# One-bank PSUM tiles in the block products of a mixture-of-experts kernel, with the row staging in two parts

## The chip, the cores and the metric

One core of one Trainium2 chip runs the whole program. The metric is device time in microseconds (us), from the program's start to its end on that core, as the median of several executions. The kernel before has a median of 686.16 us. The rows below come from one execution under the hardware profiler, whose own time was 684.45 us.

## What is computed

Linear attention without a softmax for 8 batches and 8 heads (576 rows of 64 columns), an RMS normalization of every head's row, and a mixture of experts in which each of the 4608 resulting rows of 512 columns goes to the best one of 8 experts:

```python
kv = np.einsum('bhsd,bhde->bhse', q, np.einsum('bhsd,bhse->bhde', k, v))   # then RMS norm, g_norm
x = attn_out.transpose(0, 2, 1, 3).reshape(B * S, H * D)                   # 4608 x 512
e_idx = np.argmax(x @ w_gate, axis=1)
for e in range(E):
    mask = e_idx == e
    h = np.maximum(x[mask] @ w1[e], 0.0)                                   # 512 -> 1024
    ye = h @ w2[e]                                                         # 1024 -> 512
    out[mask] = gate_w[mask, None] * eom[mask, e, None] * ye
```

All inputs and outputs are fp32, and the matrix products of the experts keep nearly that precision: an operand is split into a high and a low part (`hi`, `lo`), and a product is three matmuls (high by high, high by low, low by high).

## The kernel before

The first 110 us or so do the attention and the routing; rows are written to a buffer `xs` in DRAM, and lists of indices (`gidx`, `oidx`) say which rows an expert takes. The experts follow, ordered by their number of rows, in nine runs (`RUNS`): the first expert has two runs (256 and 436 rows), the others one each, of 672, 632, 608, 592, 576, 576 and 544 rows. A run gathers its rows, computes h (1024 x rows) and from it y, which a DMA writes to the rows of the output.

From the third run on, x @ w1 is made with Winograd's form of the 2 x 2 block product, `seven(i)`. For each of four chains c (256 of the 1024 columns of h) it issues seven products of six matmuls each (`product`, L458; two contraction blocks by three pairs of high and low parts), each n = rows / 2 columns wide. Their names are those of the operand blocks: 11, S3, 12, S2, S1 of chain c, and in between S4 and 22 of the chain before (`late3`, `late4`). Two accumulators hold a chain: `a` takes 11, S2, S1 and, while the next chain runs, S4, one on top of another; ScalarE copies its state to `sn` after the first three (L511, L521, L529). `d` takes S3 and later 22; VectorE reads it after each (L530, L496). VectorE's L518 adds the product 12 to the first of these copies. `split_h` writes a part of h: a relu on ScalarE (L482) gives the high part, VectorE (L485) the low one. The product 12 goes to one of two other banks (`y0`, `y1`), which the results of mm2 use too. `a` and `d` are the two banks of one PSUM tile:

```python
            ad = ps_b.tile([P, 2, 512], F32, name="hps", tag="big")
            a, d = ad[:, 0, 0:n], ad[:, 1, 0:n]
```

The pool `ps_b` has three such two-bank buffers; the staging of rows takes its tile `tps` from the same pool. Two banks are left for `ps_y`. The framework orders the accesses to a tile and inserts every semaphore wait; within the runs each of TensorE, ScalarE, VectorE and GpSimd executes its instructions in the order in which the program issues them.

`mm2(i, k, events)` makes y for one tile k of 128 rows: eight steps f of three matmuls of 512 columns (0.23 us each at full clock), then the evacuation by ScalarE (L588) and the indirect DMA from GpSimd (L589). The dictionary `events` hangs other work behind a step f of a tile, with `put(tile, step, function, ...)`. So while a run's mm2 is on TensorE, the next run is prepared: `sums_of` (sums of weight blocks, on GpSimd), `w_split` (high and low parts of those weights, ScalarE and VectorE), `x_stage(i + 1, k)` for k = 0, 1, 2 (two row tiles each: eight transposes on TensorE into `tps`, then copies, sums of blocks and their low parts on ScalarE and VectorE, in turns), the loads of weights (`wload`, SP's queue), and, in the last tile, the first chain of the next run. The gather of the next run's rows and `scale_rows` (GpSimd) are issued between the chains of the run before. `listing` is a list of small VectorE operations on rows that fit no expert's place; two of its pieces are issued per chain in the third and fourth run.

SBUF tiles for weights, rows and block sums come from one ring of 29 slots (`take` and `give`): whoever takes a slot waits for the last user of it.

Of the kernel before, what the change touches and what calls it, by code (L numbers as in the profile page):

```python
# [21 lines left out]
P = 128  # L22
# [113 lines left out]
def body(ctx: ExitStack, tc: tile.TileContext, kvm, rem, qT, wg, gn, w1, w2, kc, xs, tab, out):  # L136
# [24 lines left out]
    main = ctx.enter_context(ExitStack())  # L161
    mem = main.enter_context(tc.tile_pool(name="mem", bufs=1))
    psum = bass.MemoryType.PSUM
    ps_b = main.enter_context(tc.tile_pool(name="ps_b", bufs=3, space=psum))
    ps_y = main.enter_context(tc.tile_pool(name="ps_y", bufs=1, space=psum))
    loads = []
    kvp, mrp = (ps_y.tile([P, 512], F32, name=n, tag=t) for n, t in (("kvp", "y0"), ("mrp", "y1")))
    free = list(range(SLOTS - ROWS))
# [187 lines left out]

    wsum, wop, xop = {}, {}, {}

    def rest(i):

# [46 lines left out]
    def x_stage(i, k):  # L409

        p, _, C = RUNS[i]
        n, r = C // 2, rest(i)
        if k == 0:
            xop[i] = [hp.tile([P, 6, n], F32R, name=f"xb{j}") for j in range(2)]
            xop[i] += [mem.tile([P, 8, n], F32R, name="xT", tag=f"xT{j}") for j in range(2)]
        bh, bl, th, tl_ = xop[i]
        ps = ps_b.tile([P, 2, 512], F32, name="tps", tag="big")
        ts_ = tiles_of(i)
        for j, (t, c0, M) in enumerate(ts_[2 * k:2 * k + 2]):
            x = xg.pop((p, t))  # L420
            tl = cst.tile([P, 1], F32, name="tl", bufs=14)
            nc.vector.tensor_copy(tl[:M], x[:M, C_SCALE:C_SCALE + 1])
            tails[(p, t)] = tl
            for c in range(4):
                if k < 2:
                    o = ps[:, j, c * P:(c + 1) * P]
                else:
                    o = ps[:, c // 2, c % 2 * 256 + j * P:][:, 0:M]
                nc.tensor.transpose(o, x[:M, c * P:(c + 1) * P], ident[:M, :M])
            give(x)  # L430
        m, c0 = (P, k * P) if k < 2 else (r // 2, 2 * P)
        if k < 2:
            v = ps.rearrange("q b (c m a) -> q a c b m", c=4, a=2)
            part = lambda t, d: t[:, d, c0:c0 + m].rearrange("q d (b m) -> q d b m", b=2)
        else:
            v = ps.rearrange("q b (c m a) -> q a (b c) m", c=2, a=2)[:, :, :, 0:m]
            part = lambda t, d: t[:, d, c0:c0 + m]
        a, b = v[:, 0], v[:, 1]
        xt_ = take([P, 8, P], F32, "xt")
        xt = xt_[:, :, 0:m]  # L440
        if k < 2:
            xt = xt.rearrange("q d (b m) -> q d b m", b=2)
        V = nc.vector
        d1, d2 = slice(0, 2), slice(2, 4)
        nc.scalar.copy(xt[:, 6:8], b[:, d1])
        V.tensor_tensor(out=xt[:, 0:2], in0=xt[:, 6:8], in1=a[:, d1], op=ALU.subtract)
        V.tensor_tensor(out=xt[:, 4:6], in0=b[:, d2], in1=xt[:, 6:8], op=ALU.subtract)
        V.tensor_tensor(out=xt[:, 2:4], in0=b[:, d2], in1=xt[:, 0:2], op=ALU.subtract)
        V.tensor_tensor(out=xt[:, 6:8], in0=a[:, d2], in1=xt[:, 2:4], op=ALU.subtract)  # L449
        cs = slice(c0, c0 + m)  # L450
        for hi, lo, x in ((part(bh, slice(0, 4)), part(bl, slice(0, 4)), a),
                          (part(bh, slice(4, 6)), part(bl, slice(4, 6)), b[:, d2]),
                          (th[:, :, cs], tl_[:, :, cs], xt_[:, :, 0:m])):
            nc.scalar.copy(hi, x)  # L454
            V.tensor_tensor(out=lo, in0=x, in1=hi.bitcast(F32), op=ALU.subtract)  # L455
        give(xt_)

    def product(ps, W, X, start):  # L458
# [7 lines left out]
    def seven(i):  # L466

        nonlocal ny
        p, _, C = RUNS[i]
        n = C // 2  # L470
        st = {}
        S, V = nc.scalar, nc.vector

        T = half(i)
        C0 = C - T

        def split_h(c, f, a, x):

            h = hT[i][:, 2 * c + f]
            v = lambda o, k: h[:, o:o + 2 * k].rearrange("q (k a) -> q a k", a=2)[:, a]  # L480
            hh = v(0, n)
            S.activation(hh, x, AF.Relu)  # L482
            cut = C0 // 2
            for o, j0, j1 in ((C + T, 0, cut), (C, cut, n)) if T else ((C, 0, n),):
                V.scalar_tensor_tensor(out=v(o, j1 - j0), in0=x[..., j0:j1], scalar=0.0,  # L485
                                       in1=hh[..., j0:j1].bitcast(F32), op0=ALU.max, op1=ALU.subtract)

        def late3(c):
            a, d, sn, ct = st[c]
            product(a, w_of(c, "S4"), x_of(i, "22"), False)  # L490
            split_h(c, 0, 1, a)

        def late4(c):
            a, d, sn, ct = st.pop(c)
            product(d, w_of(c, "22"), x_of(i, "T4"), False)
            V.tensor_tensor(out=ct[:, 0:n], in0=d, in1=sn[:, 1], op=ALU.add)  # L496
            split_h(c, 1, slice(0, 2), ct[:, 0:2 * n].rearrange("q (a k) -> q a k", a=2))
            give(st.pop(("sn", c)))
            give(st.pop(("ct", c)))
            w_drop(c)  # L500

        for c in range(4):
            ad = ps_b.tile([P, 2, 512], F32, name="hps", tag="big")
            a, d = ad[:, 0, 0:n], ad[:, 1, 0:n]
            st["sn", c] = take([P, 1024], F32, "sn")
            st["ct", c] = take([P, 1024], F32, "ct")
            sn = st["sn", c][:, 0:3 * n].rearrange("q (s n) -> q s n", s=3)
            ct = st["ct", c][:, 0:3 * n]
            st[c] = (a, d, sn, ct)
            product(a, w_of(c, "11"), x_of(i, "11"), True)  # L510
            S.copy(sn[:, 0], a)  # L511
            yield
            product(d, w_of(c, "S3"), x_of(i, "T3"), True)
            yield
            b = ps_y.tile([P, DM], F32, name="hps2", tag=f"y{ny % 2}")[:, 0:n]
            ny += 1
            product(b, w_of(c, "12"), x_of(i, "21"), True)
            V.tensor_tensor(out=ct[:, 2 * n:3 * n], in0=b, in1=sn[:, 0], op=ALU.add)  # L518
            yield
            product(a, w_of(c, "S2"), x_of(i, "T2"), False)  # L520
            S.copy(sn[:, 1], a)  # L521
            yield
            if c:
                late3(c - 1)
                yield
                late4(c - 1)
                yield
            product(a, w_of(c, "S1"), x_of(i, "T1"), False)
            S.copy(sn[:, 2], a)  # L529
            V.tensor_tensor(out=ct[:, n:2 * n], in0=d, in1=sn[:, 2], op=ALU.add)  # L530
            if c == 0:
                hT[i] = hp.tile([P, 8, 2 * C], F32R, name="hT")
            split_h(c, 0, 0, ct[:, 2 * n:3 * n])
            yield
        late3(3)
        yield
        late4(3)
        xop.pop(i)
        yield
# [651 lines left out]
    with tc.manual_schedule(engines=MAN):  # L1191
# [12 lines left out]
        for i in range(len(RUNS)):  # L1204
# [7 lines left out]
            elif i == 1:  # L1212
                for f in range(8):
                    mm1(i, f)
                    if f % 2:
                        split(p, 2, f // 2)
                        drop(1, f // 2)
                        wload(p + 1, 1, f // 2)
                    if f == 2:
                        gather(i + 1)  # L1220
                    if f == 3:
                        scale_rows(i + 1)
                    if f == 6:
                        sums_of(p + 1, 0)
            else:

                for c in range(4):
                    if c:
                        begin(i, 6)
                        if change:  # L1230
                            wload(p + 1, 1, c - 1)
                        begin(i, 1)
                    split(p, 2, c)
                    if c == 1 and not last_run:
                        g_ = gather(i + 1)
                        if i + 2 == len(RUNS):
                            settle(g_)
                    if c == 2 and not last_run:
                        scale_rows(i + 1)
                    if c == 3 and change:  # L1240
                        sums_of(p + 1, 0)
                    next(listing, None)
                    next(listing, None)

# [11 lines left out]
                if change:  # L1256
                    put(order[0], 3, wload, p + 1, 1, 3)
            if change:
                for c in range(1, 4):
                    put(order[c - 1], 4, sums_of, p + 1, c)  # L1260
                for c in range(4):
                    put(order[min(c, T - 2)], 5 if c < T - 1 else 6, w_split, p + 1, c)
                for k in range(3):
                    put(order[k], 6, x_stage, i + 1, k)
                put(order[T - 1], 0, wload, p + 1, 2, 0)
                for f, n in ((1, 1), (3, 2), (5, 1), (7, 1)):
                    put(order[T - 1], f, begin, i + 1, n)
# [120 lines left out]
```

## Time and profile before

| | |
|---|---|
| median of the runs shown | 686.16 us |
| profiled execution, its own time | 684.45 us |
| its span, first to last instruction | 682.6 us |
| mean granted TensorE clock | 0.95 of 2.4 GHz |
| TensorE (PE) busy | 568.8 us, 83% |
| VectorE (DVE) busy | 395.1 us, 58% |
| ScalarE (ACT) busy | 293.9 us, 43% |
| GpSimd (POOL) busy | 261.8 us, 38% |

A busy share is an average over the attention, the chains and mm2, which have different limits; matmuls are pipelined, so that a busy TensorE need not be at its peak. What a change to the chains can be worth is read from the waits inside them.

### The profile page before, as it was taken

How to read it: one execution, taken by the hardware profiler on the slowest of the kernel's cores; microseconds unless marked ns; L12 is line 12 of the kernel's file. 1: busy time of each engine (PE TensorE's matmuls, PEld its weight loads, DVE VectorE, ACT ScalarE, POOL GpSimd, SP SyncE). 2: the span in 40 equal slices, each digit the busy share in tenths (PEclk: the TensorE clock that was granted, in tenths of full speed). 3: DMA queues.
4: the chain of work that ended last, by engine and by line, in shares of the span. 5: the costliest groups of instructions: out<-in, count | busy, mean ns of one | idle time of the engine just before them, and what ended most of it. 6: DMA issues, size and time to landing. Idle time of an engine off the chain costs nothing.

```text
span 682.6 us, 10867 instructions
## 1 busy us (share of the span) xinstructions
PE 568.8 (83%) x4052; PEld 476.2 (70%) x4052; DVE 395.1 (58%) x806; ACT 293.9 (43%) x583; POOL 261.8 (38%) x280
## 2 busy tenths in 40 slices
PE   8999999999487699779886978698868886888696
PEld 6888887588276577677676857676667676767674
DVE  1238988468736674547725683578256844784430
ACT  1577644235523354335524553455234533453321
POOL 2001431892425434165515461546154623662011
PEclk9899969999789999899889999997999899989999
DMA  8999988520144002341243015301530153013000
GB/s 283 385 417 415 400 335 329 179 83 16 47 146 135 32 15 94 125 138 42 72 163 119 32 62 182 118 31 62 179 119 32 57 170 122 32 52 135 1 17 39
DMA packets 28743, 92.34 MB, mean 135 GB/s; under 512 B 4082, under 2 KB 4210, under 8 KB 28688
## 3 DMA queue, kind: packets, MB, share of 16 engines
q1 hardware_dynamic: 21952, 71.63, 28.9%
q0 software_dynamic: 6304, 19.78, 8.7%
q8 instruction: 33, 0.54, 0.3%
q10 hardware_dynamic: 432, 0.21, 0.1%
q14 instruction: 22, 0.18, 0.1%
HBM read 72.41 MB, written 19.78 MB: 135 GB/s over the span
## 4 chain that ended last, share of the span: by engine, by line
PE 40%; DVE 21%; ACT 16%; issue 6%; POOL 1%; DMA 0%; POOLq 0%; ACTq 0%; DVEq 0%
PE hps L462 21%; PE yps L575 11%; DVE wl L387 6%; ACT hT L482 5%; DVE hT L485 4%; ACT whi L225 3%; PE yps L569 3%; DVE wlo L228 3%; PE hps L308 2%; PE yps L553 2%; DVE ct L496 2%; ACT y L588 2%; DVE xb L455 1%; ACT wh L386 1%; ACT xb L454 1%
## 5 line engine op out<-in xcount | busy, mean ns | idle before, releaser
L575 PE MATMUL yps<-whi,hT 128*128 128x512 f32 (+3 forms) x560 | 193.8, 410 | 18.9 <-ACT y L588 18.9
L462 PE MATMUL hps<-xT,wh 128*128 128x288 f32 (+5 forms) x448 | 101.2, 315 | 64.9 <-ACT sn L511 35.7
L575 PEld LDWEIGHTS yps<-whi,hT 128*128 128x128 f32 (+3 forms) x560 | 108.2, 193 | 47.2 <-ACT y L588 23.0
L589 POOL DMA_INDIRECT out<-y,oidx x42 | 50.7, 1207 | 226.3 <-ACT y L588 183.9
L462 PEld LDWEIGHTS hps<-xT,wh 128*128 128x128 f32 x448 | 74.2, 192 | 79.8 <-ACT sn L511 40.9
L575 PE MATMUL yps<-wlo,hT 128*128 128x512 f32 (+3 forms) x280 | 113.5, 405 | 0.1
L462 PE MATMUL hps<-xb,wh 128*128 128x288 f32 (+5 forms) x336 | 74.8, 311 | 14.0 <-ACT xb L454 8.9
L462 PEld LDWEIGHTS hps<-xb,wh 128*128 128x128 f32 x336 | 56.9, 195 | 18.4 <-ACT xb L454 9.3
L243 POOL DMA_INDIRECT xg<-xs,gidx x42 | 42.3, 1008 | 69.6 <-DVE ct L496 28.6
L462 PE MATMUL hps<-xT,wl 128*128 128x288 f32 (+5 forms) x224 | 68.4, 305 | 0.0
L482 ACT ACTIVATE hT<-ct 128x288 fp32r<-128x288 f32 (+11 forms) x56 | 34.5, 617 | 70.8 <-DVE ct L496 70.8
L485 DVE SCALAR_TENSOR_TENSOR hT<-ct,hT 128x256 fp32r<-128x256 f32 (+6 forms) x88 | 48.7, 583 | 22.9 <-ACT hT L482 22.9
L575 PEld LDWEIGHTS yps<-wlo,hT 128*128 128x128 f32 (+3 forms) x280 | 54.4, 194 | 10.7 <-DVE wlo L228 0.5
L521 ACT COPY sn<-hps 128x288 f32<-128x288 f32 (+5 forms) x28 | 11.5, 410 | 94.1 <-PE hps L462 94.1
L462 PE MATMUL hps<-xb,wl 128*128 128x288 f32 (+5 forms) x168 | 51.3, 306 | 0.0
L454 ACT CAST xb<-tps 128x512 fp32r<-128x512 f32 (+11 forms) x42 | 17.2, 409 | 77.1 <-DVE xt L449 63.6
L228 DVE TENSOR_TENSOR wlo<-wraw,whi 128x1024 fp32r<-128x1024 f32 x32 | 45.5, 1423 | 6.0 <-ACT whi L225 5.9
L259 POOL TENSOR_TENSOR xg<-xg 128x512 f32<-128x512 f32 (+6 forms) x40 | 43.3, 1113 | 12.3 <-issue 9.4
L387 DVE SCALAR_TENSOR_TENSOR wl<-wraw,gcol,wh 128x512 fp32r<-128x512 f32 (+1 forms) x56 | 44.8, 841 | 4.3 <-ACT wh L386 4.3
L387 DVE SCALAR_TENSOR_TENSOR wl<-ws,gcol,wh 128x1024 fp32r<-128x1024 f32 x28 | 42.5, 1517 | 2.9 <-ACT wh L386 2.8
L797 DVE TENSOR_REDUCE ss<-sq 128x8 f32<-128x512 f32 x36 | 23.9, 681 | 34.2 <-ACT sq L787 34.2
L771 PE MATMUL ops<-aug,ld 64*128 64x80 f32 (+1 forms) x640 | 43.0, 291 | 0.1
(201 smaller groups left out, 1008.7 us busy)
## 6 DMA issues: line engine op xcount, KB each, us to landing
wraw<-w SPq DMA_DIRECT2D x64, 512.0 KB, 4.2
ld<-kvm SPq DMA_DIRECT2D x32, 512.0 KB, 9.9
ld<-qT SPq DMA_DIRECT2D x18, 512.0 KB, 10.1
xs<-xrow SPq DMA_DIRECT2D x9, 528.0 KB, 6.2
xs<-xrow SPq DMA_DIRECT2D x2, 1320.0 KB, 7.3
xs<-xrow SPq DMA_DIRECT2D x1, 2112.0 KB, 12.5
ld<-rem SPq DMA_DIRECT2D x3, 512.0 KB, 9.9
xg<-xs,gidx POOLq DMA_INDIRECT x42, 3.9
```

The costliest lines, as they stand in the source:

```text
L228: eng.tensor_tensor(out=lo, in0=r, in1=hi.bitcast(F32), op=ALU.subtract)
L243: gathered = nc.gpsimd.indirect_dma_start(out=x[:M, :], out_offset=None, in_=rows, in_offset=bass.IndirectOffsetOnAxis(ap=gidx[:M, p, t:t ...
L259: eng.tensor_tensor(out=v, in0=v, in1=f, op=ALU.mult)
L387: nc.vector.scalar_tensor_tensor(out=lo, in0=x, scalar=gcol[:, 0:1], in1=hi.bitcast(F32), op0=ALU.mult, op1=ALU.subtract)
L454: nc.scalar.copy(hi, x)
L462: nc.tensor.matmul(ps, W[a][d], X[b][d], start=start and k == 0, stop=k == 5, skip_group_check=not start)
L482: S.activation(hh, x, AF.Relu)
L485: V.scalar_tensor_tensor(out=v(o, j1 - j0), in0=x[..., j0:j1], scalar=0.0, in1=hh[..., j0:j1].bitcast(F32), op0=ALU.max, op1=ALU.subtract)
L575: nc.tensor.matmul(ps[:M], a, b, start=(f == 0 and j == 0), stop=(f == 7 and j == 2))
L589: i_ = nc.gpsimd.indirect_dma_start(out=out, out_offset=bass.IndirectOffsetOnAxis(ap=oidx[:M, p, t:t + 1], axis=0), in_=y[:M], in_offset=N ...
L771: nc.tensor.matmul(v[r0:r0 + m, u, p, :], qt[g // 2][r, p, q0:q0 + m], augs[b % 3][r, p, :], start=True, stop=True)
L797: nc.vector.tensor_reduce(out=o, in_=sq, axis=AX.X, op=ALU.add)
```

## The change

The two halves of `ad` become tiles of one bank each, from a pool "two" with two buffers of each; the staging's tile becomes two one-bank tiles from a pool "one" with one buffer of each. Both pools are opened after the second run's mm1, in the place of `ps_b` (which closes there).

`x_stage` is cut in two. The first part makes the transposes and, bank by bank, ScalarE's three reads of the bank and then VectorE's six; the second part, `x_sums`, splits the block sums `xt`, which lie in SBUF, into high and low parts.

The order of issue is changed. In the loop over chains, the weight split of chain c comes after the chain's first two products and not behind its last one; the next run's gather comes after chain 2 in place of chain 1; `sums_of(p + 1, 0)` and `scale_rows` come after chain 3, in that order. Under mm2 the staging's first part is hung on step 2 of tiles 0, 1 and 2 (it was 6, and so behind `late3` and `late4` of the last chain, at steps 1 and 3, where now only `late3` is ahead), the second part on step 7, the weight splits on step 4 (it was 5), the later sums on step 0 (it was 4).

```diff
-    ps_b = main.enter_context(tc.tile_pool(name="ps_b", bufs=3, space=psum))
     ps_y = main.enter_context(tc.tile_pool(name="ps_y", bufs=1, space=psum))
+    wide = main.enter_context(ExitStack())
+    ps_b = wide.enter_context(tc.tile_pool(name="ps_b", bufs=3, space=psum))
...
-        ps = ps_b.tile([P, 2, 512], F32, name="tps", tag="big")
+        pss = [pools["one"].tile([P, 512], F32, name=f"tps{j}") for j in range(2)]
...
+            for a, b, xt, cs in todo:
+                A.copy(xt[:, 6:8], b[:, 0:2])
+                A.copy(bh[:, 0:4, cs], a)
+                A.copy(bh[:, 4:6, cs], b[:, 2:4])
+                V.tensor_tensor(out=bl[:, 0:4, cs], in0=a, in1=bh[:, 0:4, cs].bitcast(F32), op=ALU.subtract)
+                V.tensor_tensor(out=bl[:, 4:6, cs], in0=b[:, 2:4], in1=bh[:, 4:6, cs].bitcast(F32), op=ALU.subtract)
+                V.tensor_tensor(out=xt[:, 0:2], in0=xt[:, 6:8], in1=a[:, 0:2], op=ALU.subtract)
+                V.tensor_tensor(out=xt[:, 4:6], in0=b[:, 2:4], in1=xt[:, 6:8], op=ALU.subtract)
+                V.tensor_tensor(out=xt[:, 2:4], in0=b[:, 2:4], in1=xt[:, 0:2], op=ALU.subtract)
+                V.tensor_tensor(out=xt[:, 6:8], in0=a[:, 2:4], in1=xt[:, 2:4], op=ALU.subtract)
...
-        nc.scalar.copy(xt[:, 6:8], b[:, d1])
-        V.tensor_tensor(out=xt[:, 0:2], in0=xt[:, 6:8], in1=a[:, d1], op=ALU.subtract)
...
-            nc.scalar.copy(hi, x)
-            V.tensor_tensor(out=lo, in0=x, in1=hi.bitcast(F32), op=ALU.subtract)
...
+    def x_sums(i, k):
+
+        bh, bl, th, tl_ = xop[i]
+        xt_, m, cs = xsum.pop(k)
+        nc.scalar.copy(th[:, :, cs], xt_[:, :, 0:m])
+        nc.vector.tensor_tensor(out=tl_[:, :, cs], in0=xt_[:, :, 0:m], in1=th[:, :, cs].bitcast(F32), op=ALU.subtract)
...
-            ad = ps_b.tile([P, 2, 512], F32, name="hps", tag="big")
-            a, d = ad[:, 0, 0:n], ad[:, 1, 0:n]
+            a, d = (pools["two"].tile([P, 512], F32, name=f"hps{x}")[:, 0:n] for x in "ad")
...
+                wide.close()
+                for nm, k in (("one", 1), ("two", 2)):
+                    pools[nm] = main.enter_context(tc.tile_pool(name=f"ps_{nm}", bufs=k, space=psum))
...
                     if c:
-                        begin(i, 6)
+                        begin(i, 2)
+                        split(p, 2, c)
+                        begin(i, 4)
                         if change:
                             wload(p + 1, 1, c - 1)
                         begin(i, 1)
-                    split(p, 2, c)
-                    if c == 1 and not last_run:
+                    else:
+                        split(p, 2, c)
+                    if c == 2 and not last_run:
                         g_ = gather(i + 1)
...
-                    if c == 2 and not last_run:
+                    if c == 3 and not last_run:
+                        sums_of(p + 1, 0)
                         scale_rows(i + 1)
-                    if c == 3 and change:
-                        sums_of(p + 1, 0)
...
-                for c in range(1, 4):
-                    put(order[c - 1], 4, sums_of, p + 1, c)
                 for c in range(4):
-                    put(order[min(c, T - 2)], 5 if c < T - 1 else 6, w_split, p + 1, c)
+                    if c:
+                        put(order[c - 1], 0, sums_of, p + 1, c)
+                    put(order[c], 4 if c < T - 1 else 0, w_split, p + 1, c)
                 for k in range(3):
-                    put(order[k], 6, x_stage, i + 1, k)
+                    put(order[k], 2, x_stage, i + 1, k)
+                    put(order[k], 7, x_sums, i + 1, k)
```

## Rows read from the trace of the kernel before

**Rows 1.** The page, part 1: busy us, share of the span, instructions.

```profile
PE 568.8 (83%) x4052; PEld 476.2 (70%) x4052; DVE 395.1 (58%) x806; ACT 293.9 (43%) x583; POOL 261.8 (38%) x280
```

**Rows 2.** Waits of TensorE, 160 to 670 us: total us, times, longest.

```profile
PE hps L462 <- ACT sn L511: 35.7, 21, 2.0
PE hps L462 <- DVE hT L485: 28.9, 24, 4.0
PE yps L575 <- ACT y L588: 18.9, 9, 3.0
PE hps L462 <- ACT xb L454: 8.9, 1, 8.9
PE hps L462 <- DVE ct L530: 5.1, 7, 1.9
```

**Rows 3.** TensorE in order of time, 592-row run: start, us, [idle before, releaser].

```profile
421.76 0.44 PE L462 MATMUL hps<-xb,wh 128*128 128x296 f32 x2
...
422.58 0.44 PE L462 MATMUL hps<-xT,wh 128*128 128x296 f32 x2
...
425.40 0.54 PE L462 MATMUL hps<-xT,wh 128*128 128x296 f32 x2 [1.02 <-DVE hT L485]
...
429.68 0.54 PE L462 MATMUL hps<-xT,wh 128*128 128x296 f32 x2 [1.58 <-ACT sn L511]
...
438.53 0.54 PE L462 MATMUL hps<-xT,wh 128*128 128x296 f32 x2 [1.56 <-ACT sn L511]
...
443.08 0.54 PE L462 MATMUL hps<-xT,wh 128*128 128x296 f32 x2 [1.02 <-DVE hT L485]
```

**Rows 4.** The page, part 5: the staging's casts; busy, mean ns, idle before.

```profile
L454 ACT CAST xb<-tps 128x512 fp32r<-128x512 f32 (+11 forms) x42 | 17.2, 409 | 77.1 <-DVE xt L449 63.6
```

**Rows 5.** Busy us over the eight half-clock stretches of 178 to 612 us, summed.

```profile
sum 40.95, PE 32.29 PEld 27.24 DVE 28.77 ACT 15.37 POOL 21.54; mean PE 4.04 PEld 3.40 DVE 3.60 ACT 1.92 POOL 2.69
```

**Rows 6.** TensorE in order of time, mm2 at half and full clock.

```profile
332.63 1.05 PE L575 MATMUL yps<-whi,hT 128*128 128x512 f32 x2
...
336.54 0.62 PE L575 MATMUL yps<-whi,hT 128*128 128x512 f32 x2
337.00 0.40 PE L575 MATMUL yps<-wlo,hT 128*128 128x512 f32 x1
```

**Rows 7.** ScalarE in order of time, a chain of the 592-row run.

```profile
427.02 0.73 ACT L482 ACTIVATE hT<-ct 128x592 fp32r<-128x592 f32 x1 [2.17 <-DVE ct L496]
...
428.29 1.03 ACT L225 CAST whi<-wraw 128x1024 fp32r<-128x1024 f32 x1
429.22 0.41 ACT L511 COPY sn<-hps 128x296 f32<-128x296 f32 x1
```

**Rows 8.** VectorE in order of time, three runs.

```profile
259.63 0.26 DVE L446 TENSOR_TENSOR xt<-xt,tps 128x120 f32<-128x120 f32 x1
259.82 0.27 DVE L447 TENSOR_TENSOR xt<-tps,xt 128x120 f32<-128x120 f32 x1
...
426.52 0.47 DVE L496 TENSOR_TENSOR ct<-hps,sn 128x296 f32<-128x296 f32 x1 [1.18 <-PE hps L462]
427.78 0.78 DVE L485 SCALAR_TENSOR_TENSOR hT<-ct,hT 128x592 fp32r<-128x592 f32 x1 [0.80 <-ACT hT L482]
...
505.64 2.54 DVE L485 SCALAR_TENSOR_TENSOR hT<-ct,hT 128x512 fp32r<-128x512 f32 x2 [0.80 <-ACT hT L482]
```

**Rows 9.** Busy us of each engine in one chain, with instructions.

```profile
429.68:438.53 8.85, 6.26 (x42) 5.77 (x43) 4.19 (x7) 3.45 (x7) 7.62 (x8) 1.00 0.67 210
```

**Rows 10.** GpSimd in order of time, gather, scaling and sums.

```profile
427.26 0.96 POOL L243 DMA_INDIRECT xg<-xs,gidx  x1 [4.24 <-DVE ct L496]
...
444.80 0.74 POOL L370 TENSOR_TENSOR ws<-wraw 128x256 f32<-128x256 f32 x1 [5.95 <-issue]
...
449.40 0.73 POOL L370 TENSOR_TENSOR ws<-wraw 128x256 f32<-128x256 f32 x1
...
501.85 3.04 POOL L259 TENSOR_TENSOR xg<-xg 128x512 f32<-128x512 f32 x3
```

More of the change, by code (lines that the diff above doesn't have):

```diff
@@ L350, in body @@
     ny = 0
-    wsum, wop, xop = {}, {}, {}
+    wsum, wop, xop, xsum, pools = {}, {}, {}, {}, {}
     def rest(i):
@@ L425, in x_stage @@
                 if k < 2:
-                    o = ps[:, j, c * P:(c + 1) * P]
+                    o = pss[j][:, c * P:(c + 1) * P]
                 else:
-                    o = ps[:, c // 2, c % 2 * 256 + j * P:][:, 0:M]
+                    o = pss[c // 2][:, c % 2 * 256 + j * P:][:, 0:M]
                 nc.tensor.transpose(o, x[:M, c * P:(c + 1) * P], ident[:M, :M])
             give(x)
-        m, c0 = (P, k * P) if k < 2 else (r // 2, 2 * P)
+        xt_ = take([P, 8, P], F32, "xt")
+        A, V = nc.scalar, nc.vector
@@ L432, in x_stage @@
         if k < 2:
-            v = ps.rearrange("q b (c m a) -> q a c b m", c=4, a=2)
-            part = lambda t, d: t[:, d, c0:c0 + m].rearrange("q d (b m) -> q d b m", b=2)
-        else:
[L436 to L442, printed above, removed]
@@ L443, in x_stage @@
-        V = nc.vector
-        d1, d2 = slice(0, 2), slice(2, 4)
-        nc.scalar.copy(xt[:, 6:8], b[:, d1])
-        V.tensor_tensor(out=xt[:, 0:2], in0=xt[:, 6:8], in1=a[:, d1], op=ALU.subtract)
[L447 to L453, printed above, removed]
-            nc.scalar.copy(hi, x)
-            V.tensor_tensor(out=lo, in0=x, in1=hi.bitcast(F32), op=ALU.subtract)
+            todo = []
@@ new lines, in x_stage @@
+            for j in range(2):
+                v = pss[j].rearrange("q (c m a) -> q a c m", c=4, a=2)
+                cs = slice(k * P + j * D, k * P + (j + 1) * D)
+                todo.append((v[:, 0], v[:, 1], xt_[:, :, j * D:(j + 1) * D], cs))
+            for a, b, xt, cs in todo:
[8 more added lines that the diff above has]
+                V.tensor_tensor(out=xt[:, 6:8], in0=a[:, 2:4], in1=xt[:, 2:4], op=ALU.subtract)
@@ new lines, in x_stage @@
+            cs, m = slice(k * P, (k + 1) * P), P
+        else:
+            m = r // 2
+            cs = slice(2 * P, 2 * P + m)
+            (a1, b1), (a2, b2) = [[v[:, h] for h in range(2)] for v in
+                                  (q.rearrange("q (c m a) -> q a c m", c=2, a=2)[:, :, :, 0:m] for q in pss)]
+            xt = xt_[:, :, 0:m]
+            A.copy(xt[:, 6:8], b1)
+            A.copy(bh[:, 0:2, cs], a1)
+            A.copy(bh[:, 2:4, cs], a2)
+            A.copy(bh[:, 4:6, cs], b2)
+            V.tensor_tensor(out=bl[:, 0:2, cs], in0=a1, in1=bh[:, 0:2, cs].bitcast(F32), op=ALU.subtract)
+            V.tensor_tensor(out=xt[:, 0:2], in0=xt[:, 6:8], in1=a1, op=ALU.subtract)
+            V.tensor_tensor(out=bl[:, 2:4, cs], in0=a2, in1=bh[:, 2:4, cs].bitcast(F32), op=ALU.subtract)
+            V.tensor_tensor(out=bl[:, 4:6, cs], in0=b2, in1=bh[:, 4:6, cs].bitcast(F32), op=ALU.subtract)
+            V.tensor_tensor(out=xt[:, 4:6], in0=b2, in1=xt[:, 6:8], op=ALU.subtract)
+            V.tensor_tensor(out=xt[:, 2:4], in0=b2, in1=xt[:, 0:2], op=ALU.subtract)
+            V.tensor_tensor(out=xt[:, 6:8], in0=a2, in1=xt[:, 2:4], op=ALU.subtract)
@@ L456, in x_stage @@
+        xsum[k] = (xt_, m, cs)
+    def x_sums(i, k):
[3 more added lines that the diff above has]
+        nc.vector.tensor_tensor(out=tl_[:, :, cs], in0=xt_[:, :, 0:m], in1=th[:, :, cs].bitcast(F32), op=ALU.subtract)
         give(xt_)
```

## The prediction

> **What bounds it now.** I read the page's busy shares first, then the list of who waited for whom on TensorE, then each engine in order of time over the run of 592 rows, then the granted clock. TensorE is busy 83% of the span [rows 1], more than any other engine, and from 160 us on the program is one TensorE stream with holes in it; so the question is what ends each hole. The list answers it: 62 waits, 97.5 us, in five lines [rows 2]. 21 waits (35.7 us) end with ScalarE's copy L511, 24 (28.9) with VectorE's L485, 7 (5.1) with L530, 9 (18.9) with the evacuation L588, one (8.9) with the staging's cast L454.
>
> The first three are odd. A chain issues 11 into `a`, S3 into `d`, 12, S2 into `a`, then S4 and 22 of the chain before, then S1. The product at 429.68 is S3: it writes `d`, and waits 1.58 us for L511, which reads `a`. The one at 425.40 is 22, again into `d`, and waits 1.02 us for L485, which reads the other half, `a` [rows 3]. L530 reads `d`, and the S4 that waits for it writes `a`. No operand links them, only that `a` and `d` are two banks of one tile `ad`. The staging shows the same: ScalarE's casts L454 spend 63.6 us waiting for VectorE's L449, though the two only read the same tile [rows 4].
>
> A wait costs more than its gap. From 429.68 to 438.53 a chain takes 8.85 us. One product takes 0.82 (two starts, 421.76 and 422.58), seven 5.74; so 3.11 is lost where two gaps show 1.03 and 1.56 [rows 3]. Each adds some 0.26 us of refilling: 62 x 0.26 = 16.1. And after some of the long gaps TensorE runs at half its clock: eight stretches, 41 us, in which it was busy 32.3 us [rows 5]. At 1.2 GHz a pair of mm2's matmuls takes 1.05 us, at 2.4 GHz 0.62 [rows 6]: 41% of the 32.3 is lost, 13.2. Together 97.5 + 16.1 + 13.2 = 127 us is all that TensorE could get back.
>
> **The change, part by part.**
>
> *One-bank tiles.* `a` and `d` become tiles of their own with two buffers each, and the staging has two banks that nobody else uses. S3 no longer waits for L511, nor 22 and S4 for L485 and L530. Late next is S2, which truly needs L511, as it adds into `a`. From the second chain of a run on the copy is in time: 22, started at 425.40, makes way some 0.9 us later, at 426.3; L496 follows at 426.52, the big relu at 427.02, then two small operations, and ScalarE is free at 428.29; without the split L225 before it L511 (0.41) would end at 428.70 [rows 3, 7, 8], 2.4 us after 22, while TensorE issues S1, 11, S3, 12, 3.28 us. In the first chain an evacuation and the first split's cast still precede L511: its wait, 2.0 us at the longest [rows 2], shrinks with its refill by two products (1.64): some 0.5 left in each of seven runs, 3.5. With two buffers, 11 overwrites the `a` of two chains before, last read by L485 after S4. That L485 is what 22 waited 1.02 us for; now 22 and S1 (1.64) pass meanwhile. Slack 0.6: nothing taken, 0 to 1.2 per chain kept for the range.
>
> *The split moved into the chain.* L225 (1.03) now follows L511 on ScalarE instead of preceding it, and runs under S3 and 12; the low part L228 stands before L518 and the next L485 on VectorE. A chain loads ScalarE with 3.45 and VectorE with 4.19 us [rows 9] against TensorE's 5.74: both hide.
>
> *Staging in two parts.* For 256 rows ScalarE has six reads where it had three, VectorE twelve where it had six. The nearest rows are those of 120 elements: 0.26 to 0.27 us, one started 0.19 after the other [rows 8]; so VectorE's twelve cost 12 x 0.19 = 2.3 (two of them have 256 elements: some 2.6) up to 12 x 0.27 = 3.2; I take 2.6. ScalarE's six, at most 0.41 each [rows 7], lie in a tile of mm2 that is longer. What goes is the ping-pong of [rows 4], and with it the lateness of the evacuation, which is queued behind: I strike the 18.9 us of L588, and all but 1 us of the 8.9 in the run of 436 rows, whose third stage stood behind two weight splits and now stands ahead of them (bounds: 0 and the whole).
>
> The Trainium skill speaks against the halving: "VectorE: DVE Perf Modes", section "Rules for kernel authors", asks for few operations, since each pays its own pipeline flush. The rows show 0.19 us between starts, less than the 0.27 of one; were nothing overlapped, 3.2 us per stage would stand for 2.6, and (2) below would be 0.6 longer.
>
> *The staging ahead of late4(3), gather and scaling a chain later.* Here the change adds waits. (1) The transposes now stand on TensorE three mm2 steps into tile 0, with the tile's other steps queued behind. They need scale_rows, which on GpSimd stands behind the gather and sums_of(p+1, 0). That sum began 1.7 us after the 22 of the loop's last chain (443.08 to 444.80) and took 4.6 us beside VectorE (444.80 to 449.40); its four operations alone are 4 x 0.74 [rows 3, 10]. At equal progress it begins 17.8 us into the run (two chains 11.5, first wait 0.5, five products 4.1, and 1.7), and two scalings (1.0 each) end at 22.8 to 24.4. The transposes come up at 20.6 (three chains 17.2, first wait 0.5, nine matmuls of 0.23 by [rows 6], S4 0.82). So 2 to 4 us at equal progress, down to 0 where the sum, which now follows the last weight split, gets its slot sooner; I take 1.3: six runs, 8. (2) L496 of the last chain now queues on VectorE behind the staging's twelve: 1.0 for ScalarE's copies ahead, 2.6, L496 0.47, relu 0.73, L485 0.78 [rows 7, 8], 5.6 us after the transposes; step f=7, which reads the result, comes up 3.6 us after them (0.69 + 0.82 + 2.07). As the first bank's operations start before the second transpose is done (0.5 to 1 us), the wait is 0 to 2; taken 1.2, six runs, 7. (3) The overflow list's operations on VectorE, which made the longest L485 wait, 4.0 us [rows 2], lie before the same f=7: 5 us over two runs. The later sums move some steps within their tiles; their order against the out DMAs on GpSimd stays, and so do SP's loads.
>
> Waits kept: 3.5 + 1 + 8 + 7 + 5 = 24.5. The gain is 127 - 24.5 = 102.5, and 684.45 - 102.5 = 582 for a run like the profiled one. That execution lies 1.7 us below the median of the runs shown (686.16), so I give **583 us** for the median.
>
> **Rivals.**
>
> *VectorE and GpSimd block each other.* sums_of(0), scaling, the big L485 and the weight splits crowd into one stretch. An L485 of 0.78 us took 2.54 while GpSimd scaled (505.64) [rows 8]. If each of the nine GpSimd operations (four of 0.74, five of 1.0: 8.0 us) alternates with such an operation of 0.78, the row becomes 15; the transposes wait 7 more, f=7 1.8 more, less the 2.5 counted: 6 x 6.3 = 38 us, **621**. For it: that row. Against it: the staging's VectorE operations read PSUM. The Trainium skill, "SBUF — State Buffer", section "Who interferes with whom", has it as a rule: of a GpSimd read of SBUF and a VectorE operation with two SBUF inputs, the second blocks fully.
>
> *Two buffers are too few.* The split's L228 ahead of L485 makes 11 wait up to 0.9 + 0.26 us in 21 chains: +10 to 25, about **600**.
>
> *The waits aren't the tile's.* If S3, 22 and S4 still wait, 35.7 + 28.9 + 5.1 and 52 x 0.26 stay, 83 us, less the 3.5 of S2: **662**. Against it: three kinds of wait, all across the halves of one tile.
>
> *Slower than before.* The gather, a chain later, asks for five row slots; one issue waited 4.24 us for a slot (427.26) [rows 10]. If all five wait so, 21 us in a row, scaling ends some 20 us late, and TensorE stands at the transposes in six runs: 120 less the 8 counted, and 9 more of half clock: **704**. It decides from 18.4 us per run on (102.5 / 6 beyond the 1.3 counted). Against it: that 4.24 waited for a L496, of which a chain has one.
>
> **Chances.** Forecast 0.72, blocking 0.13, buffers 0.07, waits stay 0.04, slower 0.04. A change of this kernel is told from none at about 2% (14 us). All but the last are over 2% faster: 0.96; the last is split, within 2% 0.02 (waits near its threshold), slower 0.02. Range: downward (1), (2) at nothing and a third of the rest, 18 us, 565; upward (1) at 4 us (+16) and nine more of (2) or of evacuation waits, 608, which takes in the two buffers.
>
> **What would show it.** Right: S3, 22 and S4 without a gap; a chain near 5.8 us; S2 waiting some 0.2 to 0.5 us, in first chains only; no wait for the evacuation; 2.4 GHz from 160 us on; what is left, at the transposes (for GpSimd's scaling) and at f=7 (for VectorE). Wrong: several us per run at the transposes, or new gaps of 2 us that keep the half clock.

## The result and the profile after

| | before | after |
|---|---|---|
| median | 685.93 us | 585.13 us |
| ratio, 95% interval | | 0.8545 [0.8512, 0.8579] |
| span of the profiled execution | 682.6 us | 584.7 us |
| TensorE (PE) busy | 83% [rows 1] | 93% |

The changed kernel takes 585.1 us; 583 was predicted, with a range of 565 to 608. One of the four executions of the kernel before took 2997 us; the medians count such disturbed executions, the ratios, here and below, are taken without them. First the page of the kernel after, part 1 and the clock's line of part 2 (tenths of full speed in 40 slices):

```profile
PE 545.3 (93%) x4052; PEld 464.2 (79%) x4052; DVE 378.5 (65%) x897; ACT 299.4 (51%) x632; POOL 258.4 (44%) x280
...
PEclk9999997998999989999999999999999999799999
```

The waits of TensorE in the kernel after, 160 to 670 us (total us, times, longest), to be read against [rows 2]:

```profile
PE tps L430 <- POOL xg L260: 8.8, 8, 6.0
PE yps L596 <- ACT hT L504: 4.8, 4, 3.8
PE yps L596 <- DVE hT L507: 2.8, 4, 1.3
PE hps L484 <- DVE y L605: 2.5, 4, 0.7
PE hpsa L484 <- ACT sn L542: 1.1, 1, 1.1
PE hpsa L484 <- DVE hT L507: 0.6, 1, 0.6
PE hpsa L484 <- ACT sn L532: 0.3, 2, 0.2
PE hpsd L484 <- DVE xT L477: 0.3, 1, 0.3
```

In this kernel L484 is the product (L462 before), `hpsa` and `hpsd` are the tiles `a` and `d`, L532, L542 and L550 the three copies of `a`, L551 the second sum that VectorE reads from `d`, L504 and L507 the relu and the low part, L518 the sum behind 22, L260 the scaling, L371 to L374 the weight sums, L226 and L229 the two parts of a split, L596 mm2, L609 the evacuation. Of the 62 waits and 97.5 us of [rows 2], 25 waits and 21.2 us are left. The copy of 11, which ended 21 waits, ends two, with 0.3 us; no wait of `d` for a reader of `a` is left, and none for the evacuation. The chain itself, TensorE in the 592-row run (368.86 and 374.68 are the S2 of two chains in a row, 366.84 is S3, 370.59 is 22):

```profile
366.84 0.43 PE L484 MATMUL hpsd<-xT,wh 128*128 128x296 f32 x2
...
368.86 0.54 PE L484 MATMUL hpsa<-xT,wh 128*128 128x296 f32 x2 [0.15 <-ACT sn L532]
...
370.59 0.44 PE L484 MATMUL hpsd<-xT,wh 128*128 128x296 f32 x2
...
374.68 0.44 PE L484 MATMUL hpsa<-xT,wh 128*128 128x296 f32 x2
```

From 368.86 to 374.68 a chain takes 5.82 us, where it took 8.85 [rows 9]; seven products alone take 5.74. S3 and 22 start without a gap.

From 160 us on, half clock (1.2 GHz granted) is left in two stretches, where there were eight, 41 us [rows 5]. The columns are the length, then the busy time of PE, PEld, DVE, ACT and POOL, the granted clock, the DMA share and GB/s:

```profile
214.80:221.60 6.80, 3.99 (x10) 3.01 (x11) 5.77 (x14) 4.36 (x6) 0.20 (x1) 0.51 0.00 0
498.10:504.90 6.80, 2.98 (x11) 2.50 (x12) 1.04 (x5) 1.42 (x6) 6.72 (x9) 0.51 0.00 0
```

Both lie at the two gaps over 2 us that are left. They stand in the timeline, with what held them up (TensorE, VectorE's list, GpSimd):

```profile
210.49 1.36 DVE L1194 TENSOR_TENSOR sel<-cf,cend 128x352 f32<-128x352 f32 x1
211.88 0.93 DVE L1195 TENSOR_TENSOR sel<-sel 128x352 f32<-128x352 f32 x1
...
217.61 0.79 PE L596 MATMUL yps<-whi,hT 128*128 128x512 f32 x1 [3.84 <-ACT hT L504]
...
487.59 0.87 POOL L244 DMA_INDIRECT xg<-xs,gidx  x1 [0.30 <-DVE ct L518]
497.98 0.72 POOL L371 TENSOR_TENSOR ws<-wraw 128x256 f32<-128x256 f32 x1 [9.53 <-issue]
```

At 217.61 (third run) step f = 7 waits for the last chain; the overflow list's operations (L1186 to L1195) stood on VectorE ahead of the staging and of L518. At 497.98 (eighth run; the expectations call it the seventh) GpSimd starts its weight sum 9.5 us after the last gather was issued; in between stands only a drain of GpSimd, which the runs before it don't have. The scaling follows, and TensorE stands 6.02 us at the transposes, up to 501.92.

**The sum of it.** By the prediction's way of counting, 76.3 us of waits went; 37 waits fewer at 0.26 us of refilling make 9.6; and of the 13.2 us that half clock cost, 41% of 3.99 + 2.98 = 2.9 are left, 10.3 gone. Together 96.2 us; the spans differ by 97.9. A sixth line of the list before, one wait of 1.1 us for the evacuation (L569), is not among the five of [rows 2]; it went as well.

### The profile page after: what moved, and what is told of

Read it like the earlier page. It is cut to its first block, busy times and chain, and to the rows that moved or that the text cites. A ratio compares the mean times of both kernels' runs of the same rounds, so it can differ in the third digit from the quotient of the medians.

```text
span 584.7 us, 10991 instructions
## 1 busy us (share of the span) xinstructions
PE 545.3 (93%) x4052; PEld 464.2 (79%) x4052; DVE 378.5 (65%) x897; ACT 299.4 (51%) x632; POOL 258.4 (44%) x280
## 4 chain that ended last, share of the span: by engine, by line
PE 56%; DVE 17%; DMA 11%; ACT 7%; issue 4%; POOL 2%; POOLq 1%; SPq 0%; DVEq 0%; ACTq 0%
PE yps L596 26%; PE hpsa L484 11%; PE hpsd L484 4%; DVE hT L507 4%; DMA ld<-kvm 3%; PE hps L484 3%; PE yps L590 3%; ACT hT L504 2%; PE yps L574 2%; PE tps L430 2%; DMA xs<-xrow 2%; DMA ld<-rem 2%; DVE wlo L229 2%; DMA wraw<-w 2%; PE ops L792 2%
## 5 line engine op out<-in xcount | busy, mean ns | idle before, releaser
L596 PE MATMUL yps<-whi,hT 128*128 128x512 f32 (+3 forms) x560 | 188.7, 401 | 7.9 <-ACT hT L504 4.8
L596 PEld LDWEIGHTS yps<-whi,hT 128*128 128x128 f32 (+3 forms) x560 | 104.7, 188 | 35.6 <-ACT hT L504 7.4
L610 POOL DMA_INDIRECT out<-y,oidx x42 | 57.3, 1365 | 164.7 <-ACT y L609 119.5
L596 PE MATMUL yps<-wlo,hT 128*128 128x512 f32 (+3 forms) x280 | 110.9, 396 | 0.0
L507 DVE SCALAR_TENSOR_TENSOR hT<-ct,hT 128x256 fp32r<-128x256 f32 (+6 forms) x88 | 46.3, 557 | 22.8 <-ACT hT L504 22.8
L596 PEld LDWEIGHTS yps<-wlo,hT 128*128 128x128 f32 (+3 forms) x280 | 52.6, 188 | 9.9
L504 ACT ACTIVATE hT<-ct 128x288 fp32r<-128x288 f32 (+11 forms) x56 | 34.6, 618 | 43.0 <-DVE ct L518 43.0
L229 DVE TENSOR_TENSOR wlo<-wraw,whi 128x1024 fp32r<-128x1024 f32 x32 | 43.5, 1359 | 12.3 <-ACT whi L226 12.2
L609 ACT ACTIVATE y<-yps,tl 128x512 f32<-128x512 f32 (+3 forms) x37 | 25.3, 685 | 49.3 <-PE yps L596 19.8
L484 PE MATMUL hpsa<-xT,wh 128*128 128x288 f32 (+5 forms) x224 | 48.1, 302 | 1.5 <-ACT sn L542 1.1
L484 PE MATMUL hpsd<-xT,wh 128*128 128x288 f32 (+5 forms) x224 | 48.0, 301 | 0.3 <-DVE xT L477 0.3
L484 PE MATMUL hpsa<-xb,wh 128*128 128x288 f32 (+5 forms) x224 | 47.6, 300 | 0.6 <-DVE hT L507 0.6
L260 POOL TENSOR_TENSOR xg<-xg 128x512 f32<-128x512 f32 (+6 forms) x40 | 43.6, 1122 | 0.0
L388 DVE SCALAR_TENSOR_TENSOR wl<-wraw,gcol,wh 128x512 fp32r<-128x512 f32 (+1 forms) x56 | 40.7, 766 | 0.0
L484 PEld LDWEIGHTS hpsa<-xT,wh 128*128 128x128 f32 x224 | 37.1, 188 | 4.0 <-ACT sn L542 1.3
L484 PEld LDWEIGHTS hpsa<-xb,wh 128*128 128x128 f32 x224 | 37.2, 188 | 2.2 <-DVE hT L507 0.9
L792 PEld LDWEIGHTS ops<-aug,ld 64*128 64x128 f32 (+1 forms) x640 | 36.3, 188 | 3.1 <-issue 1.2
L484 PEld LDWEIGHTS hpsd<-xT,wh 128*128 128x128 f32 x224 | 37.2, 188 | 2.0 <-DVE xT L477 0.6
L388 DVE SCALAR_TENSOR_TENSOR wl<-ws,gcol,wh 128x1024 fp32r<-128x1024 f32 x28 | 38.1, 1360 | 0.1
## 6 DMA issues: line engine op xcount, KB each, us to landing
ld<-qT SPq DMA_DIRECT2D x18, 512.0 KB, 10.5
```

The lines of the kernel that those rows point to most:

```text
L229: eng.tensor_tensor(out=lo, in0=r, in1=hi.bitcast(F32), op=ALU.subtract)
L260: eng.tensor_tensor(out=v, in0=v, in1=f, op=ALU.mult)
L388: nc.vector.scalar_tensor_tensor(out=lo, in0=x, scalar=gcol[:, 0:1], in1=hi.bitcast(F32), op0=ALU.mult, op1=ALU.subtract)
L484: nc.tensor.matmul(ps, W[a][d], X[b][d], start=start and k == 0, stop=k == 5, skip_group_check=not start)
L596: nc.tensor.matmul(ps[:M], a, b, start=(f == 0 and j == 0), stop=(f == 7 and j == 2))
L609: nc.scalar.activation(y[:M], ps[:M], AF.Copy, scale=tl[:M, 0:1])
```

## Experiments

All ratios are to the kernel before, run on the same chip at the same time.

**Tile and order apart (e1, e2).** The kernel before with one-bank tiles alone:

```diff
-            ad = ps_b.tile([P, 2, 512], F32, name="hps", tag="big")
-            a, d = ad[:, 0, 0:n], ad[:, 1, 0:n]
+            a, d = (pools["two"].tile([P, 512], F32, name=f"hps{x}")[:, 0:n] for x in "ad")
...
-        ps = ps_b.tile([P, 2, 512], F32, name="tps", tag="big")
+        ps = pools["one"].tile([P, 2, 512], F32, name="tps")
```

> The kernel before with one edit: a and d are one-bank tiles with two buffers each; the staging keeps one two-bank tile of its own, and every order of issue is that of before. If S3, 22 and S4 waited only because a and d were one tile, their 35.7 + 28.9 + 5.1 us and 52 refills of 0.26 go, 83 us; S2 then waits for the copy behind the weight split, 0.2 us in most chains (4 to 9 us back), and the evacuation's 18.9 and the staging's 8.9 stay with their half-clock stretches: 600 to 615 us. If the orders of issue carry the gain, the waits only move to S2 and 11: 655 or more.

627.6 us, ratio 0.913 [0.905, 0.921]: 58 us of the 100 by the medians, 59 by the ratio. The first lines of its list of TensorE's waits, and then its timeline at one of them, VectorE and TensorE:

```profile
PE tps L430 <- issue: 27.9, 12, 6.8
PE hpsa L463 <- ACT xb L455: 8.3, 1, 8.3
PE hpsa L463 <- ACT sn L529: 4.2, 5, 1.2
```

```profile
435.69 0.42 DVE L456 TENSOR_TENSOR xb<-tps,xb 128x256 fp32r<-128x256 f32 x1 [0.44 <-ACT xb L455]
...
436.21 0.66 PE L430 MATMUL tps<-ident,xg 64*128 64x64 f32 x4 [2.56 <-issue]
```

Of the waits of S3, 22 and S4 for a reader of the other half, 69.7 us, none is left: one 22 waits 0.2 us for L530, which reads its own `d`. S2 waits 1.6 for its copy, and S4 4.2 for the third copy (L529) of its own `a`. The time is above the range named, since 27.9 us came up at the transposes. The trace names no releaser there, but the transposes at 436.21 start 0.1 us after VectorE's last read of the stage before, at 435.69 + 0.42: the staging now has one tile where it shared three buffers. The evacuation's waits [rows 2] are down to 2.0 us, as TensorE now stands ahead of it. So that wait had moved, not gone.

The other way round, the changed kernel with the two-bank tile:

```diff
-            a, d = (pools["two"].tile([P, 512], F32, name=f"hps{x}")[:, 0:n] for x in "ad")
+            ad = pools["two"].tile([P, 2, 512], F32, name="hps")
+            a, d = ad[:, 0, 0:n], ad[:, 1, 0:n]
```

> The changed kernel with one edit: a and d are again the two halves of one two-bank tile, still with two buffers; all orders and the staging stay. If the tile makes the waits, S3 waits again for the copy of 11, 22 for the low part and S4 for the reader of d, some 1.0 + 1.2 + 0.6 us per chain and three refills of 0.26, in 25 chains 75 us or a little less, with half-clock stretches only after longer gaps: 630 to 665 us. If buffers and orders carry the gain: under 600 us.

641.9 us, ratio 0.939 [0.932, 0.946], 57 us above the changed kernel, with the old waits in nearly the old numbers (22, 22 and 7 for 24, 21 and 7; L533 is the copy of 11, L552 the reader of `d`):

```profile
PE hps L484 <- DVE hT L507: 25.3, 22, 1.8
PE hps L484 <- ACT sn L533: 25.3, 22, 2.0
PE hps L484 <- DVE ct L552: 6.0, 7, 1.7
```

The tile is worth 57 to 59 us under either order (in e1 net of the new waits at the transposes); staging and orders are worth 40 to 44 with either tile.

**The staging: form and place (e4, e5, e6).** Three kernels on the changed one: the old form (one two-bank tile, engines in turns, one piece) on step 6; the old form on step 2; the new form on step 6.

```diff
-                    put(order[k], 2, x_stage, i + 1, k)
-                    put(order[k], 7, x_sums, i + 1, k)
+                    put(order[k], 6, x_stage, i + 1, k)    # e4, old form; e5: step 2
...
-                    put(order[k], 2, x_stage, i + 1, k)
+                    put(order[k], 6, x_stage, i + 1, k)    # e6, new form
```

> The changed kernel with the staging as before: one two-bank tile, ScalarE and VectorE in turns, block sums and their split in one piece, at step 6 of the tiles. If the evacuation was late because it is queued on ScalarE behind that staging, 18.9 us of waits come back with 9 refills and one or two half-clock stretches, and the wait for the staging's cast with up to 8.9; the waits at f = 7 (5 us now) go, as the last product 22 stands ahead again: 600 to 620 us. If those waits came of the shared tiles: 583 to 590 us.

> The changed kernel with the staging's old form (one two-bank tile of its own, ScalarE and VectorE in turns, one piece) on its new place, step 2. With the same form on step 6 TensorE stood 21.2 us at the transposes, for the one tile to be read. If the form makes that wait, it stays here, 10 to 20 us with its refills, and L518 of the last chain, queued behind the turns, adds 1 to 2 us at f = 7 in each of six runs: 605 to 620 us. If the place on step 6 made it: 585 to 592 us.

> The changed kernel with the staging's first part, in its new form, hung on step 6 again, as before; the second part stays on step 7. If the form alone carries the gain, the transposes come after the scaling has ended and late4(3) ahead of the staging: the 8.8 us at the transposes shrink to the seventh run's drain and the 7.6 at f = 7 go, 572 to 583 us. If the place carries it, the reads stand behind the weight split, the next transposes or the evacuation wait 1 to 2 us in each of 18 stages: 600 to 615 us.

| | step 6 | step 2 |
|---|---|---|
| old form | 610.7 (0.891 [0.885, 0.897]) | 615.9 (0.900 [0.897, 0.903]) |
| new form | 605.0 (0.885 [0.882, 0.887]) | 585.1 (0.855 [0.851, 0.858]) |

Neither half does it alone: the form alone gives 6 us, no more than the intervals of the two ratios leave open, the place alone costs 5, both give 25.6. The other moves of the order (gather, sums, weight splits under mm2) were not tested alone. e4's time was foreseen, its place not: no evacuation waits came back (1.6 us), but 21.2 us at the transposes. e5's time too; its waits are mostly not at the transposes but at f = 7, 24.7 us in six runs. In e6 the transposes wait for the stage before. From the lists of TensorE's waits, e5's and then e6's, and from e6's VectorE in order of time:

```profile
PE yps L575 <- ACT hT L483: 24.7, 6, 6.4
```

```profile
PE tps L430 <- DVE xt L450: 13.9, 16, 1.1
PE yps L596 <- ACT y L609: 3.8, 7, 1.3
```

```profile
284.92 2.11 DVE L388 SCALAR_TENSOR_TENSOR wl<-wraw,gcol,wh 128x512 fp32r<-128x512 f32 x2
286.95 1.75 DVE L388 SCALAR_TENSOR_TENSOR wl<-ws,gcol,wh 128x1024 fp32r<-128x1024 f32 x1
288.63 0.20 DVE L423 COPY tl<-xg 128x1 f32<-128x1 f32 x2
```

On step 6 the reads of the banks stand on VectorE behind the weight split's low parts: the transposes ran at 283.93, VectorE's first read of them began at 288.76, with 3.8 us of L388 in between. On step 2 they are ahead of them; but then L518 stands behind the staging, and in the old form that is a chain of turns which ends too late for f = 7.

**The split inside the chain (e3, e9).** The split back behind the chain; and, as a second kernel, besides that the scaling ahead of the weight sum:

```diff
-                        begin(i, 2)
-                        split(p, 2, c)
-                        begin(i, 4)
+                        begin(i, 6)
                         if change:
                             wload(p + 1, 1, c - 1)
                         begin(i, 1)
-                    else:
-                        split(p, 2, c)
+                    split(p, 2, c)
...
-                        sums_of(p + 1, 0)
                         scale_rows(i + 1)
+                        sums_of(p + 1, 0)                  # e9 alone
```

> The changed kernel with the weight split of a chain back behind its last product. The high part's cast (1.03 us) then stands before the copy of 11 on ScalarE, and that copy ends 3.4 us after 22 where S2 is due after 3.28: a wait of 0.1 to 0.3 us and a refill in some 20 chains, 588 to 595 us. If the split is hidden wherever it stands: within 2 us of the changed kernel, 583 to 588 us. If the low part ahead of the next L507 cost something where the change put it: under 583 us.

> The changed kernel with the weight split behind the chain, and besides the scaling of rows issued ahead of the first weight sum on GpSimd. With the split behind the chain alone the time was 600.7 us and TensorE waited 21.3 us at the transposes for the scaling, 2.6 in each of five runs beside the drain's 6.6. If the split's place matters because the weight sum, and with it the scaling queued behind it, waits for the ring slot that the split gives back, the 2.6 us go from all runs that the drain doesn't hold up: 584 to 589 us. If the place matters by the low part on VectorE or by the gather, the transposes still wait: 597 us or more.

e3 took 600.7 us (0.877 [0.870, 0.883]), more than any case allowed, and S2 waits only 0.9 us. The 15.6 us are elsewhere. e3's waits at the transposes, and then its GpSimd in order of time:

```profile
PE tps L430 <- POOL xg L260: 21.3, 10, 6.6
```

```profile
389.30 0.73 POOL L371 TENSOR_TENSOR ws<-wraw 128x256 f32<-128x256 f32 x1 [3.31 <-issue]
```

The weight sum is late, the scaling queued behind it is late, and the transposes wait 2.6 us in each run for it. In e9, with the scaling first, these waits are gone (one of 3.3 us, in the run with the drain), and yet it took 597.9 us (0.871 [0.865, 0.878]). VectorE and GpSimd in e9:

```profile
384.86 6.52 DVE L229 TENSOR_TENSOR wlo<-wraw,whi 128x1024 fp32r<-128x1024 f32 x1
385.25 5.04 POOL L260 TENSOR_TENSOR xg<-xg 128x512 f32<-128x512 f32 x5
```

A low part L229 that takes 1.2 to 1.3 us elsewhere (372 to 383 us of the kernel after) ends 1.1 us after the last of five scalings: it stood still for all of them. Three other low parts of e9 (199.28, 268.04, 445.23), which began 0.8 to 1.0 us before the first scaling and not 0.4, keep their 1.25 us. So the expectation's queue was right, though the time fell in the range of its other case; another price took its place.

**The rest of the gaps (e7, e8, e10, e11).** On the changed kernel: the drain issued behind the scaling (e7); besides, no list operations after the last chain (e8); on e8, the scaling ahead of the weight sum (e10), or the first stage on step 3 (e11).

```diff
-                        if i + 2 == len(RUNS):
-                            settle(g_)
                     if c == 3 and not last_run:
                         sums_of(p + 1, 0)
                         scale_rows(i + 1)
+                        if i + 2 == len(RUNS):
+                            settle(g_)
-                    next(listing, None)
-                    next(listing, None)
+                    if c < 3:                               # e8, e10, e11
+                        next(listing, None)
+                        next(listing, None)
...
-                    put(order[k], 2, x_stage, i + 1, k)
+                    put(order[k], 2 if k else 3, x_stage, i + 1, k)    # e11
```

> The changed kernel with the drain of GpSimd in the seventh run issued after the sums and the scaling, not ahead of them. If the drain makes the 6.0 us at the transposes there, these go with a refill and the half-clock stretch behind them (6.8 us at half clock, some 2.3 to 2.8 lost): 9 us less, 575 to 578 us. If the gather's slots make that wait, the scaling stays as late: 584 to 587 us.

> The same, and the overflow list's pieces are issued after the first three chains of a run only, so that none lies ahead of the last chain's L518. In the third run the list held VectorE for 3.7 us there, and f = 7 waited 1.25 and 3.84 us with a half-clock stretch behind. If the list makes these waits: 3.7 of the 5.1, refills and 2.3 to 2.8 of clock, 6 us less than with the drain moved alone, 567 to 572 us. If GpSimd's hold on VectorE makes them (two L507 of 2.30 and 1.90 us there): 574 to 578 us.

> The kernel with the drain and the list moved (573.8 us), and besides the scaling ahead of the first weight sum. What is left at the transposes is 3.7 us of waits in nine gaps for the scaling; without them and their refills of 0.26 it is 568 to 571 us, if the weight sum, which ends later, is in time for its split at step 4. If it isn't, the split and the staging behind it on VectorE come later: 574 to 580 us.

> The kernel with the drain and the list moved (573.8 us), and besides the first stage of a run's staging on step 3, behind the last product 22, not on step 2; the other two stages stay. L518 and the low part of the last chain then stand ahead of the staging on VectorE, so that the 4.6 us at f = 7 go, and the transposes come 1.5 us later, which takes most of their 3.7: 565 to 570 us. If the later first stage makes the second wait for its bank, as the staging on step 6 did: 574 to 580 us.

e7: 579.1 us (0.846 [0.844, 0.849]), just over the 575 to 578 named; the longest wait at the transposes is 0.6 us, and the half clock there is gone. 6 us, not 9: all waits together fell by 4.6, not 6, since the transposes there still wait 0.5, and the stretch at half clock held only 2.98 us of TensorE's work, of which 41%, 1.2 us, was lost. e8: 573.8 us (0.838 [0.836, 0.841]), 5.3 us less and between the two cases named. In the third run 1.7 us of waits are left at f = 7, where there were 5.1, so the list made most of them; the slow L507 there (2.30 us beside GpSimd) stays.

e10 was slower, 604.1 us (0.880 [0.874, 0.886]), 30 us more than e8 and above both cases named. The weight sum wasn't the reason. One of five such places, in e10's timeline:

```profile
449.19 6.27 DVE L507 SCALAR_TENSOR_TENSOR hT<-ct,hT 128x512 fp32r<-128x512 f32 x2 [0.80 <-issue]
449.73 5.04 POOL L260 TENSOR_TENSOR xg<-xg 128x512 f32<-128x512 f32 x5
456.02 0.67 PE L484 MATMUL hpsa<-xT,wh 128*128 128x288 f32 x2 [5.03 <-ACT sn L532]
```

An L507 of 512 columns stands still during five scalings (6.13 of the 6.27 us; the row joins it with a short second one); ScalarE's copy of 11 comes behind it, and S2 waits 5.03 us for the copy.

e11: 564.0 us (0.824 [0.820, 0.828]), just under its 565 to 570, the fastest here, 21 us under the changed kernel. All its waits, 160 to 670 us; those at f = 7 and for the scaling are gone:

```profile
PE hps L484 <- DVE y L605: 2.5, 4, 0.7
PE tps L430 <- DVE xt L450: 1.9, 3, 0.8
PE hpsa L484 <- DVE hT L507: 0.9, 2, 0.6
PE hpsd L484 <- DVE xT L477: 0.4, 1, 0.4
PE hps L484 <- ACT y L609: 0.2, 1, 0.2
PE hpsa L484 <- ACT sn L532: 0.2, 1, 0.2
```

## Why the prediction was right, and where it wasn't

**The tile.** Right: the products waited because `a` and `d` were one tile. e1 and e2 show it from both sides, 57 to 59 us. The rival "the waits aren't the tile's" (662) is out.

**S2.** Mechanism right, size wrong: 3.5 us were counted for the copy of 11 in first chains; 0.3 were measured, in two second chains (368.86, 424.56).

**The split moved into the chain.** "Both hide" was right for what the split costs and missed what it does. Its place gives 15.6 us (e3), and not through ScalarE's copy: it gives back the ring slot for which the weight sum, and behind it the scaling, waits. The slot appeared in (1) in half a sentence only, as a lower bound. That it is the slot rests on e3's and e9's rows, the order of the queue and the releaser of L371 in the kernel after (L229, five times, 14.6 us); no run gave the sum a slot of its own. Once the split did not hide: in the fourth run its cast L226 waited 2.80 us for its weights to land (257.41), the second copy of `a` (L542) stood behind it on ScalarE, and S1 waited the 1.1 us of the list.

**The staging.** The evacuation's 18.9 us and the cast's 8.9 went, as struck. But the reason given, the end of the turns, is half of it: without the new place the wait for the bank takes over (e6). The prediction had counted the place as a cost alone, (1) and (2). The price of the twelve halved operations was right. VectorE after:

```profile
388.43 0.42 DVE L445 TENSOR_TENSOR xb<-tps,xb 128x256 fp32r<-128x256 f32 x1 [1.32 <-ACT xb L444]
388.77 0.28 DVE L446 TENSOR_TENSOR xb<-tps,xb 128x128 fp32r<-128x128 f32 x1
388.97 0.28 DVE L447 TENSOR_TENSOR xt<-xt,tps 128x128 f32<-128x128 f32 x1
...
391.33 0.45 DVE L518 TENSOR_TENSOR ct<-hpsd,sn 128x296 f32<-128x296 f32 x1
```

From 388.43 to 391.33 the twelve take 2.9 us (2.6 taken, 2.3 to 3.2 the bounds).

**Terms (1), (2) and (3).** (1), 8 us at the transposes: 8.8 measured, but 6.0 of it is the drain in one run, which the prediction passed over; the scaling's place costs 2.8 in seven gaps, not 1.3 per run. (2) and (3), 12 us at f = 7: 7.6 measured, 5.1 of it in the third run, behind the list (e8). Not foreseen at all: product 12 waits four times, 2.5 us, for VectorE's L605, which reads its bank `y` in the evacuation of a half tile. In all, kept waits are 21.2 us with 6.5 of refilling and 2.9 of clock, 30.6, against 24.5: the 4.5 us by which the profiled execution (586.47) missed 582, to within 2. That the number came so near is in part luck: the terms foreseen measured 10.7 us of waits (0.3 at S2, 2.8 and 7.6), and 10.5 of others came in their place (6.0 behind the drain, 2.5 of product 12, 2.0 in three smaller waits).

**Two buffers.** 11 waited once, 0.6 us, for the low part of two chains before: enough.

**Blocking.** The rival's mechanism is real, and the order kept its price small. In the changed kernel the weight sum stands first, and in the 592-row run the five scalings go from 385.68 to 390.95, where VectorE does the staging: the rows above, each with an operand in PSUM, keep their 0.28 us. Where an L507 does meet the scaling there, the two take turns, as the rival let them. The worst place, VectorE and GpSimd in the third run:

```profile
204.59 2.30 DVE L507 SCALAR_TENSOR_TENSOR hT<-ct,hT 128x640 fp32r<-128x640 f32 x2 [0.88 <-ACT hT L504]
205.20 6.26 POOL L260 TENSOR_TENSOR xg<-xg 128x512 f32<-128x512 f32 x5
```

The pair of L507 takes 0.93 us at 217.59, the five scalings 5.04 elsewhere. Two L229 in e9 and five L507 in e10 (one row of each stands above) were held through three to five scalings. e10 took 30 us more than e8, and e9 9 to 14 more than expected; how much of e9's surplus the hold makes was not measured apart. For those orders the rival's size was wrong. The 2.54 us it started from [rows 8] are two operations in one row, of 1.56 and 1.06. What decides between a turn and a hold is open: the seven held operations began beside the last gather, less than 0.6 us before the first scaling, the L507 here beside the weight sum, and the three low parts of e9 that began beside the gather but earlier were not held. The Trainium skill, "SBUF — State Buffer", section "Who interferes with whom", has the condition (two SBUF inputs beside a GpSimd read), and the rows of these seven agree; a cast with one input (L1206) was held as well, once, 4.45 us for 0.19 (e10, at 270.07). The same section of the Trainium skill says that the order of issue decides who blocks. In e9 and e10 the VectorE operations began 0.4 to 0.5 us before the scaling and were held by it (6.52 and 6.13 us), so for this case the measurement decides.

**Gather slots.** The slower rival didn't come: GpSimd did wait at the gathers (up to 3.1 us, at 371.84), but the transposes' waits are explained without that, by the drain (e7) and the scaling's place.

## What to carry to other kernels

Where an engine waits for a reader of data that it doesn't touch, look at what the two share, and split the tile before anything else. A wait that goes tells little until the next one in line is known: the staging's wait moved from evacuation to transposes to f = 7 as its form, its place and its buffers changed, and only form and place together removed it. Keep GpSimd's long runs of SBUF operations beside VectorE work that reads PSUM, and drains off the path to the next stage.

## What the runs showed of the hardware

A VectorE operation with two SBUF inputs that meets five back-to-back GpSimd operations of 1.0 us can be held through three to five of them: seven took 4.1 to 6.5 us for work of 0.2 to 1.3 (e9, e10), and a cast with one input 4.45 for 0.19 (e10). It need not be: in the changed kernel such operations got their turn after one at most (2.30 us for a pair of 0.93). VectorE operations with an operand in PSUM keep their 0.28 us beside the same scalings. With only a drain of GpSimd between an indirect gather and the weight sum, 9.5 us passed, where the sum waits up to 3.2 us in the runs without one; with the scaling issued ahead of the drain, 6.4 us passed behind it (e7).
